# A fused attention and two-MLP kernel: the lower words of 22 weight slots, several half-precision copies and the first value splits on GpSimd, and a new order

## The chip, the cores and the metric

The kernel runs on one core of a Trainium2 chip. The metric is device time in microseconds. A core has TensorE (PE in the profile), VectorE (DVE), ScalarE (ACT), GpSimd (POOL), and SyncE (SP), which issues the DMA transfers. Each engine works through its own queue of instructions in order; semaphores tie the queues together.

## The reference, cut to what matters

```
# q, k, v: (4, 8, 576, 64); window 128
scores = scale * q @ k^T + ALiBi bias, masked to 0 <= i-j < 128
attn   = softmax(scores);  x = attn @ v               # (2304, 512) after the heads are joined
h      = x @ w_in                                      # 512 -> 1024
solu   = h * softmax(h);  ln = (solu - mean) / sqrt(var + 1e-6) * g_ln
y      = ln @ w_out                                    # 1024 -> 512
h2     = y @ w2_in;  g = h2 * sigmoid(h2)              # 512 -> 2048
out    = g @ w2_out                                    # 2048 -> 512
```

The weights arrive as 64-bit floats, so each number is two 32-bit words in memory.

## The kernel before, in words

The 2304 rows are 18 blocks of 128 (index i). Two blocks are a chunk (c, nine of them). A block goes through scores (`a_qk`, TensorE, L688), row maximum (`a_max`, L714 on DVE, read from PSUM), exponential (L719, ACT), splitting of the probabilities into two half-precision parts (`a_parts`: a copy L342 on ACT or L343 on DVE, then a subtraction L354 on DVE or L355 on POOL), a transposing DMA, the product with the values (`a_av`, L773), the first MLP (`m1_in` L820, `layer_norm`, and per chunk `m1_out` L920), and per chunk the second MLP in eight steps (`m2_in` L957, a tanh L966 on ACT, L967 on DVE, a copy L969 on ACT, L970 on DVE, and `m2_out` L984).

Each product of two numbers is made of three half-precision products: high by high, high by low, low by high. That is why every operand is split in a high part (a copy) and a low part (a subtraction).

Weights fill 48 slots of 128x512 in `W`: 0 to 7 hold w_in, 8 to 15 w_out, 16 to 31 w2_in, 32 to 47 w2_out. A slot is loaded as pairs of 32-bit words into `stage` (one transfer of 512 KB, five buffers in all), then decoded to 32-bit floats (`decode`): ACT works on the higher words (L456), DVE scales the lower words to three bits (L458), and DVE joins both into `W` (L460). 46 slots go this way, two another (L464 to L468). Then TensorE and DVE find a norm, and `split_weight` scales the slot and splits it in half-precision parts: scale L347 on ACT, L348 on DVE or L350 on POOL; copy L342 or L343; subtraction L354 or L355; or, in the slots marked V in `E_W`, scale and fused subtraction L533. The values of a block are scaled and split by `v_split`: a scaled copy (L347 or L348) and a fused subtraction on DVE (L642).

The order of all of this is fixed before the program is emitted. `Sched.solve` gives every operation an engine and a place by priorities (`RANK`, `SLOPE`, `LATER`: a number for each kind of step and block), by costs written in the code, and by the strings in `PICK` that name the engine of each copy, scale and subtraction. Operations whose entry ends in True are kept apart in that plan: two such operations on DVE and POOL are never planned at once. The join L460 does not carry that mark.

Of the kernel before, what the change touches and what calls it, by code (L numbers as in the profile page):

```python
# [298 lines left out]
def fused_kernel(ctx, tc, qk, qn, kn, vt, rel, w_in, w_out, g_ln, w2_in, w2_out, out):  # L299
# [60 lines left out]
    def transpose(fn, r=(), w=(), blocks=8):  # L360
        s.op([("SP", 1294, fn, False)], r, w, dma=165 * blocks)
# [81 lines left out]
    def decode(st, slot, j):  # L443
# [4 lines left out]
        def high():  # L448
            return st[:, :, 1]
# [186 lines left out]
    def v_split(i):  # L636
# [3 lines left out]
        r = vraw[i]  # L640
        scaled(("vh", i), 512, lambda: t[:, :, 0, :], lambda: r.tile, lambda: sv.tile, [r, sv], [(t, 0)])
# [182 lines left out]
    def layer_norm(i):  # L824
# [120 lines left out]
    def m2_in(c, j):  # L945
# [18 lines left out]
        def flat(x):  # L964
# [3 lines left out]
                                              op1=ALU.mult), [t, pt], [t])  # L968
        act(512, lambda: A.activation(flat(g[:, 0]), t.tile, AF.Copy, scale=2.0 ** -16), [t], [(g, 0)])  # L969
# [77 lines left out]
    n = 0  # L1047
    for c in range(NB // 2 + 1):
# [7 lines left out]
        while n < until:  # L1056
# [12 lines left out]
RANK = {"aturn": 8190.5, "av": 1566.9, "evac": -3109.3, "exp": 5884.2, "gate": -1711.8, "in": -283.0, "in2": 763.1,  # L1069
        "load": -4397.6, "lparts": -1653.6, "max": 176.2, "max1": 339.6, "norm": -7961.4, "out": -1027.6,  # L1070
        "out2": 3298.4, "parts": -1379.1, "qk": 1402.7, "s0": -168.5, "s16": 369.8, "s32": 455.6, "s8": 3931.6,
        "share": -1605.8, "store": 2439.7, "table": -5196.2, "tav": 59.2, "tevac": -749.8, "texp": 4157.2,
        "tpar": 3201.3, "tscore": -1216.6, "tsub": 333.9, "vload": 753.3, "vnorm": -2520.6, "vsplit": 128.2,
        "w0": 1479.2, "w16": 76.9, "w32": 998.7, "w8": -63.2, "xturn": -869.5, "y": -1911.0}
SLOPE = {"aturn": 47.79, "av": -25.89, "evac": -5.68, "exp": 11.77, "gate": -21.88, "in": 36.34, "in2": -11.62,
         "load": 10.3, "lparts": 18.87, "max": -24.94, "max1": -2.34, "norm": -4.0, "out": 15.06, "out2": 30.48,
         "parts": -23.26, "qk": 32.18, "s0": 3.76, "s16": 1.95, "s32": 6.94, "s8": 26.54, "share": 17.85,
         "store": -34.37, "table": 17.51, "tav": -5.62, "tevac": 7.06, "texp": 19.15, "tpar": 25.04, "tscore": 5.66,
         "tsub": 13.31, "vload": 7.87, "vnorm": 15.99, "vsplit": 25.91, "w0": -6.05, "w16": 1.69, "w32": -8.51,
         "w8": -8.24, "xturn": 39.68, "y": -12.6}  # L1080
# [148 lines left out]
```

## Time and profile before

| what | us |
|---|---|
| median of three runs | 732.65 |
| the three runs | 731.47, 732.65, 2431.59 |
| the profiled execution, its own time | 729.44 |
| its span, first to last instruction | 727.5 |
| busy in the span: TensorE, DVE, ACT, POOL | 674.3, 444.8, 346.2, 138.5 |
| mean granted TensorE clock | 0.981 of full |

The median is that of the two runs that agree within 1.2 us and one far outlier above them. The profiled execution's own time lies 1.9 us over its span, and 3.2 us under the median.

### The profile page before, as it was taken

To read this page: it belongs to the slowest core of one execution; us is meant where nothing else is said; L and a number is where in the kernel's file an instruction comes from. 1 tells how busy PE (TensorE), PEld (TensorE's weight loads), DVE (VectorE), ACT (ScalarE), POOL (GpSimd) and SP (SyncE) were. 2 spreads that over 40 slices of the span, in tenths; PEclk is the share of its full clock that TensorE was granted. 3 is DMA by queue.
4 is the path that set the end of the run, shared out by engine and by line. 5 is a ranking of instruction groups with operands and counts; after the bars stand their busy time and mean duration, and the time that the engine had idled before them with its cause. 6 is when DMAs were issued, how large, how long until landed. Compare 5 with 4: busy or idle time off the path is not lost.

```text
span 727.5 us, 13956 instructions
## 1 busy us (share of the span) xinstructions
PE 674.3 (93%) x5541; PEld 464.0 (64%) x5541; DVE 444.8 (61%) x1125; ACT 346.2 (48%) x738; POOL 138.5 (19%) x140
## 2 busy tenths in 40 slices
PE   4563688999999999999999999999999999999997
PEld 2432367778565577667766676678566777657853
DVE  3899999996897747553556657547672523321220
ACT  5687668575646635444454445525341422231231
POOL 1223034322443312130322112101010200100000
PEclk9996799999999999999999999999999999999999
DMA  9999985593535534251723454334250421100000
GB/s 309 346 247 273 241 199 134 131 231 89 99 78 103 130 73 81 53 114 31 145 59 73 82 107 90 91 56 73 44 102 1 68 65 30 30 30 1 1 30 29
DMA packets 142209, 75.82 MB, mean 104 GB/s; under 512 B 126656, under 2 KB 126784, under 8 KB 142144
## 3 DMA queue, kind: packets, MB, share of 16 engines
q1 hardware_dynamic: 142144, 74.94, 44.2%
q8 instruction: 43, 0.70, 0.4%
q14 instruction: 22, 0.18, 0.1%
HBM read 39.52 MB, written 4.72 MB: 61 GB/s over the span
## 4 chain that ended last, share of the span: by engine, by line
PE 79%; DVE 14%; ACT 3%; issue 2%; DMA 1%; POOL 0%; DVEq 0%; POOLq 0%; ACTq 0%
PE mm L984 25%; PE mm L957 23%; PE mm L920 12%; PE mm L820 11%; PE sa L688 4%; DVE W L460 3%; PE mm L773 2%; DVE stage L458 2%; DVE e L714 1%; PE gram L396 1%; DVE W L533 1%; PE sa L773 1%; DVE W L354 1%; DMA aT<-a 1%; DVE W L348 1%
## 5 line engine op out<-in xcount | busy, mean ns | idle before, releaser
L957 PE MATMUL mm<-y,W 128*128 128x256 f16 x1728 | 210.4, 273 | 1.1 <-DVE t L967 0.7
L984 PE MATMUL mm<-W,g 128*128 128x512 f16 x864 | 204.9, 379 | 0.0
L957 PEld LDWEIGHTS <-W 128*128 128x128 f16 x1728 | 167.0, 98 | 39.8 <-issue 2.0
L984 PEld LDWEIGHTS <-g 128*128 128x128 f16 x864 | 81.8, 98 | 78.7 <-issue 0.2
L820 PE MATMUL mm<-W,xT 128*128 128x512 f16 x432 | 105.2, 390 | 1.7 <-DVE xT L569 1.0
L920 PE MATMUL mm<-lnT,W 128*128 128x256 f16 x864 | 104.8, 273 | 0.0
L920 PEld LDWEIGHTS <-W 128*128 128x128 f16 x864 | 84.0, 98 | 19.7 <-issue 0.5
L719 ACT ACTIVATE e<-e,mx 128x256 f32<-128x256 f32 (+1 forms) x144 | 70.0, 487 | 45.9 <-DVE mx L714 43.3
L970 DVE SCALAR_TENSOR_TENSOR g<-t,g 128x512 f16<-128x512 f32 x72 | 55.5, 774 | 53.7 <-ACT g L969 53.3
L355 POOL TENSOR_TENSOR a<-e,a 128x512 f16<-128x512 f32 (+1 forms) x45 | 54.9, 1222 | 143.2 <-ACT a L342 65.8
L969 ACT ACTIVATE g<-t 128x512 f16<-128x512 f32 x72 | 45.0, 626 | 72.6 <-PE mm L984 61.1
L967 DVE SCALAR_TENSOR_TENSOR t<-t,mm 128x512 f32<-128x512 f32 x72 | 48.7, 682 | 48.3 <-ACT t L966 48.3
L966 ACT ACTIVATE t<-mm,cs 128x512 f32<-128x512 f32 x72 | 48.1, 680 | 62.5 <-PE mm L957 58.6
L820 PEld LDWEIGHTS <-xT 128*128 128x128 f16 x432 | 42.7, 100 | 47.6 <-issue 4.6
L688 PE MATMUL sa<-k,q 64*128 64x128 f32 x544 | 49.4, 312 | 17.1 <-DVE mx L714 12.2
L714 DVE CUSTOM_DVE_ANT_0 e<-sa,table 128x256 f32<-128x256 f32 (+1 forms) x144 | 53.9, 400 | 11.3 <-PE sa L688 6.3
L688 PEld LDWEIGHTS sa<-k,q 64*128 64x128 f32 x544 | 38.5, 202 | 29.1 <-DVE mx L714 15.7
L928 DVE SCALAR_TENSOR_TENSOR y<-mm,cs,y 128x512 f16<-128x512 f32 x18 | 13.3, 748 | 57.1 <-ACT y L925 57.1
L834 DVE TENSOR_REDUCE lnst<-mm 128x1 f32<-128x1024 f32 x18 | 22.0, 1220 | 42.0 <-PE mm L820 42.0
L848 POOL TENSOR_SCALAR lnst<-lnst 128x1 f32<-128x1 f32 x17 | 3.5, 203 | 214.0 <-ACT mm L845 214.0
L925 ACT ACTIVATE y<-mm,cs 128x512 f16<-128x512 f32 x18 | 12.2, 686 | 64.0 <-PE mm L920 56.3
L773 PEld LDWEIGHTS <-aT 128*128 128x128 f16 x816 | 32.9, 101 | 15.2 <-issue 8.6
(151 smaller groups left out, 707.9 us busy)
## 6 DMA issues: line engine op xcount, KB each, us to landing
stage<-in_moe_w_in_dram SPq DMA_DIRECT2D x24, 512.0 KB, 5.3
stage<-in_moe_w_out_dram SPq DMA_DIRECT2D x24, 512.0 KB, 4.5
k<-in_kn_dram SPq DMA_DIRECT2D x18, 256.0 KB, 2.9
q<-in_qn_dram SPq DMA_DIRECT2D x18, 256.0 KB, 3.1
vraw<-in_vt_dram SPq DMA_DIRECT2D x18, 256.0 KB, 3.8
out_dram<-t SPq DMA_DIRECT2D x18, 256.0 KB, 2.3
aT<-a SPq DMA_TRANSPOSE x72, 3.3
lnT<-ln SPq DMA_TRANSPOSE x34, 3.2
```

The source lines that it names most:

```text
L355: ("G", cg(n), lambda: G.tensor_tensor(dst(), a(), b(), op), True)], r, w, pick=pick)
L688: T.matmul(SA[:, j, off + sl * P:off + (sl + 1) * P], q[rows, p, :], k[rows, p, :], start=True, stop=sl not in blank)
L714: v(n + 20, lambda j=j: V.tensor_tensor_reduce(e[:, j, lo:lo + n], SA[:, j, off + lo:off + lo + n], table[:, 2 * p + j, o:o + n], -0.125, ...
L719: act(n, lambda j=j: A.activation(e[:, j, lo:lo + n], e[:, j, lo:lo + n], AF.Exp, bias=mx[:, j:j + 1], scale=-1.0, accum_out=rs[:, 2 * p + ...
L773: T.matmul(heads(i)[:, h // 4, h % 4, :], t[:, (2 * ha + j) * nh + c, :], vb[sl][:, h, hv, :], start=(n == 0), stop=(n == 3 * nh - 1))
L820: T.matmul(pt[:, half * 512:(half + 1) * 512], x[:, hx, k, :], W16(2 * k + half, hw), start=(k == 0 and hx + hw == 0), stop=(k == KD - 1 a ...
L920: T.matmul(pt[:, ct % 2], W16(8 + k, hw)[:, ct * P:(ct + 1) * P], l[:, hx * KF1 + k, :], start=(k == 0 and hw + hx == 0), stop=(k == KF1 - ...
L957: T.matmul(pt[:, mm], W16(16 + 4 * k + m // 4, hw)[:, (m % 4) * P:(m % 4 + 1) * P], y[:, hx, k, :], start=(k == 0 and hw + hx == 0), stop= ...
L966: act(512, lambda: A.activation(t.tile, flat(pt.tile), AF.Tanh, scale=cs[:, 0:1]), [pt, (cs, 0)], [t], extra=1)
L967: v(512, lambda: V.scalar_tensor_tensor(out=t.tile, in0=t.tile, scalar=1.0, in1=flat(pt.tile), op0=ALU.add, op1=ALU.mult), [t, pt], [t])
L970: v(512, lambda: V.scalar_tensor_tensor(out=flat(g[:, 1]), in0=t.tile, scalar=2.0 ** -16, in1=flat(g[:, 0]), op0=ALU.mult, op1=ALU.subtrac ...
L984: T.matmul(pt.tile, g[:, hg, mm, b * P:(b + 1) * P], W16(32 + m, hw), start=(m == 0 and hg + hw == 0), stop=(m == KF2 - 1 and hg == 1))
```

## The change

The lower words may be scaled by GpSimd (L461 of the changed kernel): the string `wd` gives 22 slots to it, one of which is in the pair that is decoded the other way, so 21 instructions move. Copies to half precision may go to GpSimd as a multiplication by one (L344): 21 of them do. The values of blocks 0 to 5 are split in three steps instead of two: scaled in place, copied, subtracted, most of it on GpSimd. A branch for the gate is added and not used (`GATE` is all V). All numbers of the order are new; some engines in `PICK`, `ROOT`, `NORM` and `E_W` are, too, and `V_AT` starts the norms of the third and fourth batch at blocks 6 and 8, not 9 and 10. Costs in the plan change with them. TensorE's instructions are the same ones, 10245 in both.

```diff
     def copy(pick, n, dst, src, r, w):
 
         s.op([("A", ca(n), lambda: A.activation(dst(), src(), AF.Copy), False),
-              ("V", cv(n, True), lambda: V.tensor_copy(dst(), src()), True)], r, w, pick=pick)
+              ("V", cv(n, True), lambda: V.tensor_copy(dst(), src()), True)] +
+             ([("G", cg1(n), lambda: G.tensor_scalar(dst(), src(), 1.0, 1.0, ALU.mult, ALU.mult), True)]
+              if pick[0] in ("wh", "ah", "xh", "lh", "vg") else []), r, w, pick=pick)
...
-            v(512, lambda: V.tensor_scalar(low(), low(), 2.0 ** -29, 7.0, ALU.mult, ALU.min), [(st, 0)],
-              [(st, "low")], fast=True)
-            v(530, lambda: V.scalar_tensor_tensor(out=out(), in0=high(), scalar=3, in1=low(),
+            s.op([("V", cv(615, True), lambda: V.tensor_scalar(low(), low(), 2.0 ** -29, 7.0, ALU.mult, ALU.min), True),
+                  ("G", cg1(560), lambda: G.tensor_scalar(low(), low(), 2.0 ** -29, 7.0, ALU.mult, ALU.min), True)],
+                 [(st, 0)], [(st, "low")], pick=("wd", j))
+            v(582, lambda: V.scalar_tensor_tensor(out=out(), in0=high(), scalar=3, in1=low(),
                                                   op0=ALU.logical_shift_left, op1=ALU.bitwise_or),
...
+        if V_SPLIT[i] == "G":
+            scaled(("vc", i), 512, lambda: r.tile, lambda: r.tile, lambda: sv.tile, [r, sv], [r], True)
+            copy(("vg", i), 512, lambda: t[:, :, 0, :], lambda: r.tile, [r], [(t, 0)])
+            combine(("vl", i), 512, ALU.subtract, lambda: t[:, :, 1, :], lambda: r.tile, lambda: t[:, :, 0, :],
+                    [r, (t, 0)], [(t, 1)])
+            return
...
-RANK = {"aturn": 8190.5, "av": 1566.9, "evac": -3109.3, "exp": 5884.2, "gate": -1711.8, "in": -283.0, "in2": 763.1,
+RANK = {"aturn": 7491.5, "av": 1875.4, "evac": -3132.7, "exp": 6823.8, "gate": -2780.3, "in": -507.5, "in2": 1352.2,
...
+PICK = {"vc": "AVVGAAAAAAAAAAAAAA", "vg": "GGAAGVAAAAAAAAAAAA", "vl": "GGGGGVGGGGGGGGGGGG",
...
+        "wd": "VVVVGVVVGGGVGVGVGVGVGVGVGVGVGVGVGVGVGVGVGVGGGVVV",
...
+V_SPLIT = "GGGGGGVVVVVVVVVVVV"
+GATE = "VVVVVVVVV"
 V_NORM = "PPAA"
-V_AT = [0, 1, 9, 10]
+V_AT = [0, 1, 6, 8]
```

How the order moves is shown at three places. The lines of the changed kernel are shifted: its L460 scales lower words on DVE, L461 on POOL, L463 joins, L350 scales, L356 and L357 subtract, L723 is the row maximum, L976 the step that was L967.

DVE, the first weights and values, before (`stage` is a loaded slot, `vraw` the values of a block, `vs` their parts):

```order
L458 TENSOR_SCALAR stage_76<-stage_76 128x512
L642 SCALAR_TENSOR_TENSOR vs_150<-vraw_170,sv0_160,vs_150 128x8x64
L642 SCALAR_TENSOR_TENSOR vs_149<-vraw_169,sv0_160,vs_149 128x8x64
L460 SCALAR_TENSOR_TENSOR W_188<-stage_76 128x512
L458 TENSOR_SCALAR stage_82<-stage_82 128x512
L460 SCALAR_TENSOR_TENSOR W_188<-stage_82 128x512
L458 TENSOR_SCALAR stage_230<-stage_230 128x512
L460 SCALAR_TENSOR_TENSOR W_188<-stage_230 128x512
```

DVE, the same place in the changed kernel:

```order
L350 TENSOR_SCALAR vraw_171<-vraw_171,sv0_160 128x512
L350 TENSOR_SCALAR vraw_170<-vraw_170,sv0_160 128x512
L586 COPY sv_4_94<-sv0_160 64x1
L463 SCALAR_TENSOR_TENSOR W_188<-stage_81 128x512
L460 TENSOR_SCALAR stage_76<-stage_76 128x512
L460 TENSOR_SCALAR stage_82<-stage_82 128x512
L463 SCALAR_TENSOR_TENSOR W_188<-stage_76 128x512
L463 SCALAR_TENSOR_TENSOR W_188<-stage_82 128x512
L460 TENSOR_SCALAR stage_77<-stage_77 128x512
L463 SCALAR_TENSOR_TENSOR W_188<-stage_77 128x512
L343 CAST a16_351<-e_247 128x256
L463 SCALAR_TENSOR_TENSOR W_188<-stage_223 128x512
```

The fused value subtractions are gone from DVE, and the join of `stage_223` has no scaling ahead of it on DVE.

POOL, from its first subtraction on, before (`a16` are parts of probabilities, `e` the probabilities, `x16` and `xm` the joined heads):

```order
L355 TENSOR_TENSOR a16_138<-e_145,a16_138 128x256
L355 TENSOR_TENSOR a16_359<-e_254,a16_359 128x256
L350 TENSOR_SCALAR W_188<-W_188,swin_155 128x512
L355 TENSOR_TENSOR a16_463<-e_376,a16_463 128x512
L355 TENSOR_TENSOR a16_482<-e_385,a16_482 128x512
L355 TENSOR_TENSOR x16_133<-xm_134,x16_133 128x512
```

POOL, the same stretch in the changed kernel, up to the scaling of a w_in slot:

```order
L357 TENSOR_TENSOR vs_149<-vraw_169,vs_149 128x8x64
L344 TENSOR_SCALAR vs_150<-vraw_170 128x8x64
L357 TENSOR_TENSOR vs_150<-vraw_170,vs_150 128x8x64
L461 TENSOR_SCALAR stage_223<-stage_223 128x512
L357 TENSOR_TENSOR a16_351<-e_247,a16_351 128x256
L461 TENSOR_SCALAR stage_359<-stage_359 128x512
L461 TENSOR_SCALAR stage_377<-stage_377 128x512
L344 TENSOR_SCALAR a16_473<-e_384 128x512
L352 TENSOR_SCALAR W_188<-W_188,swin_155 128x512
```

Two subtractions stood before the scaling of that slot; now there are thirteen instructions, of which the last eight are shown.

DVE at the seventh step L967 of the second MLP, before (the joins around it are those of the last weight slots):

```order
L714 ISA e_1941,mx_1602<-sa_75,table_187 128x256
L714 ISA mx_1602 128x1
L458 TENSOR_SCALAR stage_1886<-stage_1886 128x512
L468 SCALAR_TENSOR_TENSOR W_188<-stage_1820,W_188 128x512
L967 SCALAR_TENSOR_TENSOR t_1723<-t_1723,mm_1910 128x512
L460 SCALAR_TENSOR_TENSOR W_188<-stage_1886 128x512
```

DVE at the seventh such step in the changed kernel (its L976):

```order
L723 ISA e_2029,mx_1888<-sa_75,table_187 128x256
L723 ISA mx_1888 128x1
L976 SCALAR_TENSOR_TENSOR t_1782<-t_1782,mm_1953 128x512
L792 TENSOR_SCALAR rinv_1452<-rsum_896 128x8
L793 RECIPROCAL rinv_1452<-rinv_1452 128x8
L467 TENSOR_SCALAR W_188<-stage_1991 128x512
L469 SCALAR_TENSOR_TENSOR W_188<-stage_1991,W_188 128x512
L471 SCALAR_TENSOR_TENSOR W_188<-stage_1991,W_188 128x512
L976 SCALAR_TENSOR_TENSOR t_1793<-t_1793,mm_2021 128x512
```

The last of these L976 is the seventh. In both orders all but the last joins of weights stand ahead of it, and nearly the same number of matrix products that can start before it: 894 before, 910 in the change.

## Rows read from the trace of the kernel before

**Rows 1.** The page, busy tenths in 40 slices of the span: TensorE and DVE.

```profile
PE   4563688999999999999999999999999999999997
DVE  3899999996897747553556657547672523321220
```

**Rows 2.** Stretches: us, then busy us (instructions) by engine, granted clock, DMA share, GB/s.

```profile
0.00:20.00 20.00, 7.87 (x53) 5.72 (x53) 8.30 (x38) 12.37 (x33) 2.42 (x15) 1.00 0.97 313
20.00:160.00 140.00, 103.44 (x911) 72.81 (x911) 134.57 (x340) 99.18 (x205) 40.83 (x38) 0.90 0.85 225
160.00:700.00 540.00, 539.28 (x4462) 373.74 (x4463) 297.18 (x741) 228.32 (x492) 95.28 (x87) 1.00 0.34 69
700.00:727.00 27.00, 23.70 (x122) 11.73 (x120) 4.74 (x7) 6.31 (x10) 0.00 (x0) 1.00 0.10 39
```

**Rows 3.** Waits: engine line <- releaser: us in total, times, longest.

```profile
PE sa L688 <- DVE mx L714: 12.2, 11, 3.9
...
PE mm L773 <- DMA aT<-a: 0.5, 1, 0.5
...
DVE e L714 <- PE sa L688: 1.6, 2, 1.3
```

**Rows 4.** Order of time, 155 to 166 us, DVE and TensorE: start, us, what.

```profile
160.01 0.67 DVE L967 SCALAR_TENSOR_TENSOR t<-t,mm 128x512 f32<-128x512 f32 x1
...
161.23 0.82 PE L920 MATMUL mm<-lnT,W 128*128 128x256 f16 x6
```

**Rows 5.** DVE by line and form, 0 to 160 us: count, busy us, mean ns.

```profile
L460 DVE SCALAR_TENSOR_TENSOR W<-stage 128x512 uint32<-128x512 uint32 x44 | 34.5, 795 | 0.9 <-ACT stage L456 0.4
L458 DVE TENSOR_SCALAR stage<-stage 128x512 uint32<-128x512 uint32 x45 | 21.7, 489 | 0.0
L714 DVE CUSTOM_DVE_ANT_0 e<-sa,table 128x256 f32<-128x256 f32 x34 | 13.5, 413 | 2.8 <-PE sa L688 1.6 <-PE sa L773 1.2
L354 DVE TENSOR_TENSOR W<-W 128x512 f16<-128x512 f32 x10 | 8.2, 816 | 0.0
L533 DVE SCALAR_TENSOR_TENSOR W<-W,sw2in 128x512 f16<-128x512 f32 x6 | 5.8, 986 | 0.4 <-ACT W L347 0.4
...
L642 DVE SCALAR_TENSOR_TENSOR vs<-vraw,sv,vs 128x512 f16<-128x512 f32 x5 | 3.6, 739 | 0.0
...
L343 DVE CAST a<-e 128x512 f16<-128x512 f32 x6 | 3.3, 543 | 0.0
```

**Rows 6.** The tiles W and stage: duration ns min/median/max, first and last start.

```profile
L460 DVE SCALAR_TENSOR_TENSOR W<-stage x46: 670/680/2049, 16.0 to 167.1; 128x512 uint32<-128x512 uint32 x46
L354 DVE TENSOR_TENSOR W<-W x16: 673/679/1666, 40.4 to 222.8; 128x512 f16<-128x512 f32 x16
L355 POOL TENSOR_TENSOR W<-W x16: 1152/1162/2067, 46.6 to 211.4; 128x512 f16<-128x512 f32 x16
L533 DVE SCALAR_TENSOR_TENSOR W<-W,sw2in x6: 734/747/1640, 115.6 to 140.3; 128x512 f16<-128x512 f32 x6
L348 DVE TENSOR_SCALAR W<-W,sw2out x6: 473/478/887, 178.6 to 206.4; 128x512 f32<-128x512 f32 x3, 128x512 f16<-128x512 f32 x3
...
L458 DVE TENSOR_SCALAR stage<-stage x46: 367/417/1380, 15.4 to 166.2; 128x512 uint32<-128x512 uint32 x46
```

**Rows 7.** POOL's one-input scaling L350: duration ns min/median/max, first and last start.

```profile
L350 POOL TENSOR_SCALAR W<-W,sw2in x2: 848/848/849, 107.7 to 108.6; 128x512 f32<-128x512 f32 x2
L350 POOL TENSOR_SCALAR W<-W,swin x1: 1088/1088/1088, 33.2 to 33.2; 128x512 f32<-128x512 f32 x1
L350 POOL TENSOR_SCALAR W<-W,gs x1: 686/686/686, 59.9 to 59.9; 128x512 f32<-128x512 f32 x1
```

**Rows 8.** Order of time from 107.4 to 110.4 us, POOL and DVE.

```profile
107.75 1.68 POOL L350 TENSOR_SCALAR W<-W,sw2in 128x512 f32<-128x512 f32 x2 [0.79 <-DVE q L1024]
...
108.07 1.63 DVE L348 TENSOR_SCALAR W<-W,sw2in 128x512 f32<-128x512 f32 x2
```

More of the change, by code (lines that the diff above doesn't have):

```diff
@@ L360, in transpose @@
     def transpose(fn, r=(), w=(), blocks=8):
[L361 removed]
+        s.op([("SP", 1340, fn, False)], r, w, dma=165 * blocks)
     W = Buf(const, [P, NSLOT + LAG, 512], F32, "W")
@@ L849, in layer_norm @@
                                                                ALU.add), False)], [st], [st])
-            s.op([("G", 500, lambda: G.tensor_tensor(y(), var(), half.tile, ALU.pow), False)], [st, half], [st])
+            s.op([("G", 600, lambda: G.tensor_tensor(y(), var(), half.tile, ALU.pow), False)], [st, half], [st])
         else:
@@ L968, in m2_in @@
                                               op1=ALU.mult), [t, pt], [t])
+        if GATE[c] == "G":
+            s.op([("G", cg1(512), lambda: G.tensor_scalar(t.tile, t.tile, 2.0 ** -16, 1.0, ALU.mult, ALU.mult), True)], [t], [t])
+            act(512, lambda: A.activation(flat(g[:, 0]), t.tile, AF.Copy), [t], [(g, 0)])
+            combine(("gl", 8 * c + j), 512, ALU.subtract, lambda: flat(g[:, 1]), lambda: t.tile, lambda: flat(g[:, 0]),
+                    [t, (g, 0)], [(g, 1)])
+            return
         act(512, lambda: A.activation(flat(g[:, 0]), t.tile, AF.Copy, scale=2.0 ** -16), [t], [(g, 0)])
@@ L1068 @@
 PITCH = 3.3
-RANK = {"aturn": 8190.5, "av": 1566.9, "evac": -3109.3, "exp": 5884.2, "gate": -1711.8, "in": -283.0, "in2": 763.1,
[L1070 to L1080, printed above, removed]
@@ new lines @@
+RANK = {"aturn": 7491.5, "av": 1875.4, "evac": -3132.7, "exp": 6823.8, "gate": -2780.3, "in": -507.5, "in2": 1352.2,
+        "load": -2824.7, "lparts": -3034.5, "max": 84.6, "max1": 392.4, "norm": -8853.1, "out": -1490.3,
+        "out2": 3717.9, "parts": -2273.7, "qk": 3081.3, "s0": -306.0, "s16": 481.0, "s32": 328.1, "s8": 2710.1,
+        "share": -2261.1, "store": 1605.4, "table": -4240.8, "tav": -557.6, "tevac": -1278.1, "texp": 3785.6,
+        "tpar": 2319.1, "tscore": -1263.8, "tsub": -212.9, "vload": 44.4, "vnorm": -3148.1, "vsplit": 223.5,
+        "w0": 2109.6, "w16": 57.9, "w32": 1362.9, "w8": -131.9, "xturn": -879.3, "y": -2860.6}
@@ new lines @@
+SLOPE = {"aturn": 47.89, "av": -22.61, "evac": -14.72, "exp": -2.87, "gate": -24.33, "in": 25.61, "in2": -11.6,
+         "load": 28.66, "lparts": 27.36, "max": -22.88, "max1": -16.17, "norm": 22.54, "out": 15.38, "out2": 35.04,
+         "parts": -16.75, "qk": 33.9, "s0": 10.1, "s16": -14.11, "s32": 9.76, "s8": 3.0, "share": -4.92,
+         "store": -24.87, "table": 14.8, "tav": 16.37, "tevac": 14.98, "texp": 13.48, "tpar": 20.69, "tscore": 10.69,
+         "tsub": 26.39, "vload": 10.76, "vnorm": 13.38, "vsplit": 28.36, "w0": 2.86, "w16": 12.75, "w32": 0.21,
+         "w8": -9.8, "xturn": 21.02, "y": -16.83}
```

98 lines of the change are left out of this document (49 added, 49 removed), and 41 rows, old and new, of the table LATER.

## The prediction

> **What bounds the kernel now.** I read the slices of the page first, then stretches of the span, then the waits, then the DVE groups of the first stretch. In the slices [rows 1] TensorE is at 9 tenths or more from the eighth slice to the last but one; DVE is at 9 in slices three to nine and falls to half and less later. The stretches give that in numbers [rows 2]: from 160 to 700 us TensorE is busy 539.28 of 540 us, and of its waits there the longest is 0.5 us, for a transposing DMA [rows 3]. So the last 567 us are TensorE's, its instructions are the same in both kernels, and nothing that happens on other engines there can shorten them. The time is decided by when TensorE becomes full. From 20 to 160 us it is busy 103.44 of 140 us while DVE is busy 134.57 of 140 [rows 2], and its largest wait is for DVE's row maxima, 12.2 us [rows 3]; DVE's own largest wait in that stretch is 1.6 us [rows 3]. **DVE bounds the first 160 us.**
>
> A landmark ties this to the two orders: the seventh step L967 of the second MLP, which DVE ended at 160.01 + 0.67 = 160.68 us; 0.55 us later TensorE goes on with `m1_out` and does not starve again [rows 4]. In both orders all but the last weight joins stand ahead of this step, and 894 and 910 matrix products can start before it, so it is the same point of the work. How much earlier DVE gets there is what the change is worth; the 567 us behind it are added unchanged, the last 3.3 us without TensorE (27.00 less 23.70, rows 2) too.
>
> **The change on DVE up to the landmark.** Counted in the two orders, with durations that no neighbour stretched.
> - Lower words: 45 become 23, at the median of 417 ns [rows 6]: 22 x 0.417 = -9.2 us (21 go to POOL, one moves behind the landmark).
> - Fused value subtractions: 5 become 0, at 739 ns [rows 5]: -3.7 us.
> - Value scalings on DVE: one becomes two, at 473 ns [rows 6]: +0.5 us.
> - Probability parts: one subtraction more, at some 0.68 us as L354 [rows 6], two copies fewer, at most 0.54 us each [rows 5] and, one of them being of half size, some 0.7 us in all: 0.
> - Row maxima: six more of 413 ns [rows 5] stand ahead of the landmark, with the reading of the result that follows each, together 3.0 us. This is block work that is moved forward.
>
> Sum: -9.2 - 3.7 + 0.5 + 3.0 = **-9.4 us**. ScalarE was busy 99.18 of 140 us [rows 2] and up to the landmark it loses nine instructions (copies, value scalings, one decoding step) and gains twelve of like size (six of them exponentials): nothing, covered by its 40 idle us; without that cover the three that are over.
>
> **The change on POOL up to the landmark.** The form of the 21 lower words, 32-bit whole numbers with a step of two, doesn't appear on POOL in the trace. The nearest rows are the one-input scalings L350, 686 ns alone and up to 1088 ns [rows 7]; I take 0.69, since the longer ones lie beside DVE work, and 1.09 is the other end (8.4 us more of POOL). 21 x 0.69 = 14.5; ten copies of full size at 0.69 = 6.9 and two of half size at some 0.45 = 0.9; five value subtractions at 1.16 [rows 6] = 5.8; two more probability subtractions, 2.3. One value scaling comes and one weight scaling goes. **Together +30.4 us**, on an engine that was busy 2.42 + 40.83 = 43.3 us of these 160 [rows 2]. It has room; the question is what it does to DVE.
>
> **What POOL costs DVE.** L460 takes 680 ns at the median, 2049 at most [rows 6], and 795 in the mean of this stretch [rows 5]. L458 takes 417 and 489, L354 679 and 816, L533 747 and 986. The row maximum, which reads PSUM, is not stretched: 413 mean. In order of time the stretched ones lie beside POOL: two scalings L348 took 1.63 us together while two L350 ran [rows 8], against 2 x 0.473 alone [rows 6], 0.68 us more. So a DVE operation between SBUF tiles waits until the one on POOL ends. What was lost that way: L460 44 x (795 - 680) = 5.1 us, L458 45 x 72 = 3.2, L354 10 x 137 = 1.4, L533 6 x 239 = 1.4: 11.1 us, for 43.3 us of POOL, or 0.26 us for each us of POOL. L460 alone, the one group that the plan does not keep apart from POOL, lost 5.1 / 43.3 = 0.12. So the new 30.4 us of POOL cost DVE between 30.4 x 0.12 = 3.6 us (the plan keeps the others apart) and 30.4 x 0.26 = 7.9 (they collide as the old ones did). The nearest rows to the new instructions are the four L350 of this stretch: 0.68 us lost beside two of them, nothing noted beside the others, in 1.70 + 1.09 + 0.69 = 3.5 us [rows 7, 8], 0.2. I take 30.4 x 0.2 = **+6.1 us**.
>
> The Trainium skill has the rule behind this: "SBUF — State Buffer", section "SBUF: two separate sides", says that VectorE and GpSimd hold one pair of ports as an exclusive lock for a whole instruction, and "Perfetto Trace Analysis", section "Optimizing Scalar/DVE Operations", warns that moving work between these two "might not help". The trace agrees on the lock (0.68 us lost beside L350). Taken to its end, with every new us of POOL kept from DVE, the rule would turn -3.3 into +21.0 us; by the rows it stays at -3.3.
>
> **What else is moved.** The joins of 21 slots now wait for POOL as well as for ScalarE. Behind a waiting join stands all of DVE, and behind that TensorE's scores and norms. Cover: in the new order POOL's lower word stands several DVE instructions ahead of its join (the join of stage 223 is the last of the twelve rows shown of the new order). I cost it at 0; without the cover a join waits for one POOL subtraction and the scaling, 1.16 + 0.69 us, at most, which for a fifth of the 21 would be 8 us. SP's queue keeps its transfers and gets a new order; DVE waited for no load in the rows, so 0, with the weights' loads as what comes next if DVE runs ahead.
>
> **Sum.** -9.4 + 6.1 = -3.3 us. On the profiled execution: 729.44 - 3.3 = 726.1, with a span near 724. That execution lies 3.2 us under the median of the runs, and the measurement is one of runs: 732.65 - 3.3 = **729.3 us**, 0.5% less. A change of under 2% (14.7 us) is about what a measurement of this kernel can't tell from none.
>
> **Rivals.**
> 1. *POOL's work hides.* The plan puts the new instructions where DVE reads PSUM, and no further us is lost. For it: row maxima, reductions and the MLP steps on PSUM are not stretched, and of POOL's 43.3 us before, 32 delayed none of the groups above. Against: L460, 30 us of the stretch, isn't kept apart. Time: 732.65 - 9.4 = 723.3; if part of the 11.1 us lost now goes as well, with a third of it, 719.6. Chance 0.26.
> 2. *The shared access becomes the bound* (slower). Before, DVE's groups that stretch (L460 29.9 us, L458 18.8, L354 6.8, L533 4.5, L642 3.6, L343 2.5, unstretched) and POOL's 43.3 make 109 us of 160. After, 109 - 13 + 30 = 127 in a stretch that should be 151 long. It decides from the point where DVE pays more than 9.4 / 30.4 = 0.31 us for each us of POOL; if it pays all of it, the loss is 30.4 - 9.4 = 21.0. Halfway, +10.5: 743. For it: the lock leaves only 24 us for everything that has to line up, on two engines whose queues can't be reordered. Against: at today's 0.26 it is not reached. By the skill's rule, an exclusive lock, this is the case if the plan does not hold in time. Chance 0.17.
> 3. *Joins wait for POOL.* The price above, 8 us, turns -3.3 into +4.7: 737. For it: POOL's queue had two subtractions ahead of the first w_in scaling and now has thirteen instructions. Against: POOL is busy 74 us of 151. Chance 0.07.
>
> **How the numbers follow.** Forecast 0.50 (726 to 733, the two bounds of POOL's price: 732.65 - 9.4 + 3.6 = 726.9 and + 7.9 = 731.2, with 1 us of scatter between runs, as 731.47 and 732.65 show). Rival 1 reaches from 714 to 724, rival 2 from 735 to 753, rival 3 from 733 to 741. The range 718 to 742 leaves out the lower third of rival 1 and the upper half of rival 2, under 0.2 together. Faster by over 2%, under 718.0: that third of rival 1 and a little of the forecast, 0.11. Slower by over 2%, over 747.3: a third of rival 2, 0.06. Within: 0.83.
>
> **What would show it.** Right: TensorE without waits from about 157 us on; the seventh of the former L967 ending near 157; joins (L463) with a mean above 795 ns; POOL busy over 70 us up to there; lower words on POOL near 0.7 us where DVE reads PSUM. Wrong if DVE shows idle time before the joins with POOL as releaser (rival 3), if joins and scalings on DVE show means far above 1 us (rival 2), if their means fall to 700 or less (rival 1), or if a lower word on POOL takes over 1.1 us by itself, which no row here excludes. It would also be wrong if the new order made TensorE wait behind the landmark, where it now waits under 1 us.

## The result and the profile after

The changed kernel takes **741.0 us** (median of four runs, 738.67 to 743.59); the kernel before, beside it, 732.28 us. The ratio is 1.0124, 95% interval [1.0081, 1.0167]: 8.7 us slower, within 2% but beyond what these runs leave in doubt. (One of the four runs of before took 2431.59 us; the ratio leaves it out, and the median of the other three, 731.92, makes the difference 9.1 us.) The profiled execution took 741.23 us with a span of 739.5.

Here are the slices of the page, busy tenths in 40 slices of the span, for the engines of [rows 1], and with them GpSimd and TensorE's granted clock:

```profile
PE   3554669889999999999999999999999999999997
...
DVE  3898899887599745753658468466572432422220
...
POOL 2686667744256121130314022100110200100000
PEclk9995589989999999999999999999999999999999
```

TensorE is full from the tenth slice on, where it was full from the eighth. In the fourth and fifth slices its granted clock stands at 5 tenths, near the lower of its two levels, 1.2 GHz, after three slices in which it was busy 3 to 5 tenths; in the kernel before, those two slices read 6 and 7.

The same in stretches of the span (us, then busy us and instructions of PE, PEld, DVE, ACT and POOL, granted clock, DMA share, GB/s), cut at the landmark:

```profile
0.00:20.00 20.00, 7.20 (x49) 5.23 (x49) 7.87 (x34) 12.12 (x32) 6.86 (x21) 1.00 0.91 298
20.00:174.80 154.80, 109.18 (x951) 77.44 (x951) 136.88 (x331) 103.33 (x214) 104.18 (x73) 0.86 0.77 210
160.00:700.00 540.00, 538.94 (x4502) 376.90 (x4500) 303.65 (x760) 232.50 (x498) 108.26 (x96) 1.00 0.36 73
```

And the kernel before, from 20 us to its landmark:

```profile
20.00:160.68 140.68, 104.12 (x920) 73.33 (x919) 135.25 (x342) 99.51 (x206) 40.83 (x38) 0.90 0.85 225
```

The landmark, the seventh step of the second MLP (now L976), in order of time:

```profile
174.12 0.68 DVE L976 SCALAR_TENSOR_TENSOR t<-t,mm 128x512 f32<-128x512 f32 x1
```

It ends at 174.80 us, 14.1 us after the 160.68 of before [rows 4]. Behind it nothing has happened: TensorE is busy 538.94 of 540 us (539.28 before, [rows 2]), and what lies between the landmark and the end of the span fell from 727.5 - 160.68 = 566.8 to 739.5 - 174.80 = 564.7 us. So the whole loss is ahead of the landmark; since the rest is 2.1 us shorter, the landmark stands that much further on in the work of the new order, and 14.1 counts 2.1 too many. (The profiled execution of before took 729.44 us, 2.8 under its median here; so 12.0 us between the spans stand beside 8.7 between the medians.)

Of the two columns that count there, DVE is busy about as long as before, 136.88 us against 135.25; its idle time went from 140.68 - 135.25 = 5.4 to 154.80 - 136.88 = 17.9 us. The lower clock, 0.86 in this stretch against 0.90, is not what costs the time: a kernel of the next section has 0.86 there too and does not lose. GpSimd's work up to the landmark went from 2.42 + 40.83 = 43.3 us ([rows 2] and the stretch above) to 6.86 + 104.18 = 111.0 us: **+67.8**, not +30.4.

What makes it so long stands in the rows of the tile `stage` (duration in ns, least, median, most):

```profile
L463 DVE SCALAR_TENSOR_TENSOR W<-stage x46: 672/692/1643, 18.0 to 182.8; 128x512 uint32<-128x512 uint32 x46
L460 DVE TENSOR_SCALAR stage<-stage x25: 368/422/1375, 16.0 to 182.3; 128x512 uint32<-128x512 uint32 x25
...
L461 POOL TENSOR_SCALAR stage<-stage x21: 1975/2049/2506, 21.4 to 167.7; 128x512 uint32<-128x512 uint32 x21
```

A lower word on GpSimd takes 2049 ns at the median and never under 1975. DVE's waits from 20 us to the landmark (us in total, times, longest) name GpSimd, which had no such row before:

```profile
DVE W L463 <- POOL stage L461: 4.5, 5, 1.9
...
DVE W L343 <- POOL W L357: 1.3, 1, 1.3
DVE e L723 <- POOL a L357: 1.1, 1, 1.1
```

With three more (1.1, 0.7 and 0.5 us) DVE waits 9.2 us for results of GpSimd, of which the joins are half.

And in order of time around 42 us, first GpSimd, then DVE (start, duration, what, in brackets the idle time before it and its releaser):

```profile
41.55 7.20 POOL L461 TENSOR_SCALAR stage<-stage 128x512 uint32<-128x512 uint32 x3
```

```profile
41.67 1.12 DVE L356 TENSOR_TENSOR W<-W 128x512 f16<-128x512 f32 x1
43.62 1.73 DVE L463 SCALAR_TENSOR_TENSOR W<-stage 128x512 uint32<-128x512 uint32 x2 [0.83 <-POOL stage L461]
45.27 0.68 DVE L356 TENSOR_TENSOR W<-W 128x512 f16<-128x512 f32 x1
46.20 0.69 DVE L463 SCALAR_TENSOR_TENSOR W<-stage 128x512 uint32<-128x512 uint32 x1 [0.25 <-POOL stage L461]
```

Three lower words stand in a row on GpSimd, 7.2 us of them; DVE does what it can, then stands 0.83 and 0.25 us before the joins of these slots, and all that is queued behind the joins with it.

### The profile page after: what moved, and what is told of

Read it like the earlier page. It is cut to its first block, busy times and chain, and to the rows that moved or that the text cites. A ratio compares the mean times of both kernels' runs of the same rounds, so it can differ in the third digit from the quotient of the medians.

```text
span 739.5 us, 13994 instructions
## 1 busy us (share of the span) xinstructions
PE 677.1 (92%) x5539; PEld 467.0 (63%) x5541; DVE 442.6 (60%) x1099; ACT 346.8 (47%) x732; POOL 208.4 (28%) x182
## 4 chain that ended last, share of the span: by engine, by line
PE 78%; DVE 5%; POOL 4%; ACT 3%; issue 1%; POOLq 0%; DVEq 0%
PE mm L999 25%; PE mm L966 25%; PE mm L929 11%; PE mm L829 10%; PE sa L697 4%; PE mm L782 2%; POOL stage L461 1%; POOL W L357 1%; DVE e L723 1%; DVE W L463 1%; PE sa L782 1%; ACT e L728 1%; ACT stage L458 0%; DVE ln L343 0%; POOL a L357 0%
## 5 line engine op out<-in xcount | busy, mean ns | idle before, releaser
L985 DVE SCALAR_TENSOR_TENSOR g<-t,g 128x512 f16<-128x512 f32 x72 | 57.2, 795 | 58.3 <-ACT g L984 58.0
L357 POOL TENSOR_TENSOR a<-e,a 128x512 f16<-128x512 f32 (+1 forms) x43 | 54.8, 1276 | 83.7 <-DVE a L343 44.1
L976 DVE SCALAR_TENSOR_TENSOR t<-t,mm 128x512 f32<-128x512 f32 x72 | 48.9, 682 | 49.0 <-ACT t L975 49.0
L697 PE MATMUL sa<-k,q 64*128 64x128 f32 x544 | 51.0, 319 | 23.6 <-DVE mx L723 16.0
L723 DVE CUSTOM_DVE_ANT_0 e<-sa,table 128x256 f32<-128x256 f32 (+1 forms) x144 | 53.8, 401 | 17.4 <-PE sa L697 12.1
L461 POOL TENSOR_SCALAR stage<-stage 128x512 uint32<-128x512 uint32 x21 | 44.7, 2130 | 10.6 <-ACT stage L458 5.3
L463 DVE SCALAR_TENSOR_TENSOR W<-stage 128x512 uint32<-128x512 uint32 x46 | 39.7, 872 | 5.9 <-POOL stage L461 4.5
```

The costliest lines, as they stand in the source:

```text
L357: ("G", cg(n), lambda: G.tensor_tensor(dst(), a(), b(), op), True)], r, w, pick=pick)
L461: ("G", cg1(560), lambda: G.tensor_scalar(low(), low(), 2.0 ** -29, 7.0, ALU.mult, ALU.min), True)],
L697: T.matmul(SA[:, j, off + sl * P:off + (sl + 1) * P], q[rows, p, :], k[rows, p, :], start=True, stop=sl not in blank)
L723: v(n + 20, lambda j=j: V.tensor_tensor_reduce(e[:, j, lo:lo + n], SA[:, j, off + lo:off + lo + n], table[:, 2 * p + j, o:o + n], -0.125, ...
L976: v(512, lambda: V.scalar_tensor_tensor(out=t.tile, in0=t.tile, scalar=1.0, in1=flat(pt.tile), op0=ALU.add, op1=ALU.mult), [t, pt], [t])
L985: v(512, lambda: V.scalar_tensor_tensor(out=flat(g[:, 1]), in0=t.tile, scalar=2.0 ** -16, in1=flat(g[:, 0]), op0=ALU.mult, op1=ALU.subtrac ...
```

## The experiments

All ratios are against runs of the kernel before on the same chip, whose median there was 732.2 to 732.4 us. Six kernels, those of the second and third question below, keep the changed kernel's order and alter one form, or the engine of some instructions at the places where they stand; those are the ones that tell causes apart.

**Why is a lower word 2 us long?** The theories were the 32-bit whole numbers, the step of two words, and the neighbour on DVE. The first kernel adds scalings to the changed kernel's last chunk, where DVE has little to do, on a tile of zeros of its own:

```diff
+            pr = Buf(const, [P, FF1], F32, "e1", N_E1)
...
+            for fn in (
+                lambda: G.tensor_scalar(even(U32), even(U32), 2.0 ** -29, 7.0, ALU.mult, ALU.min),
+                lambda: G.tensor_scalar(even(F32), even(F32), 2.0 ** -29, 7.0, ALU.mult, ALU.min),
+                lambda: G.tensor_scalar(flat(U32), flat(U32), 2.0 ** -29, 7.0, ALU.mult, ALU.min),
+                lambda: G.tensor_scalar(flat(F32), flat(F32), 2.0 ** -29, 7.0, ALU.mult, ALU.min),
...
+                lambda: G.tensor_scalar(even(U32), even(U32), 2.0 ** -29, 1.0, ALU.mult, ALU.mult),
```

> The changed kernel with 24 more GpSimd scalings on a tile of zeros in the last chunk, three of each of eight forms, where GpSimd has nothing else to do. Theory A (the lower words cost what they do because the words are whole numbers): the form of the change, 32-bit whole numbers with a step of two, takes 2.0 us as in the changed kernel, the same on floats 0.7 us, and whole numbers without a step 2.0 us too. Theory B (the step of two costs it): floats with a step of two take 2.0 us, whole numbers without a step 0.7. Theory C (the neighbours on VectorE stretch it): every form takes 0.7 us alone. The time of the whole is that of the changed kernel, 741 us, by all of them, since GpSimd's queue ends there.

Measured, by line of that kernel in the order of the lines shown (`even` is every second word, `flat` 512 in a row; ns least, median, most):

```profile
L1005 POOL TENSOR_SCALAR e<-e x3: 1989/2002/2016, 634.3 to 638.5; 128x512 uint32<-128x512 uint32 x3
L1006 POOL TENSOR_SCALAR e<-e x3: 1981/1992/1997, 640.5 to 644.7; 128x512 f32<-128x512 f32 x3
L1007 POOL TENSOR_SCALAR e<-e x3: 1917/1918/1919, 646.7 to 650.7; 128x512 uint32<-128x512 uint32 x3
L1008 POOL TENSOR_SCALAR e<-e x3: 1918/1918/1919, 652.7 to 656.7; 128x512 f32<-128x512 f32 x3
L1012 POOL TENSOR_SCALAR e<-e x3: 646/650/653, 677.9 to 679.4; 128x512 uint32<-128x512 uint32 x3
```

None of the three: floats, whole numbers, spread or in a row, all take 1.9 to 2.0 us with hardly a neighbour. (The three forms whose rows are left out, with mixed types and signed numbers, have medians of 1.99 us.) The last row has the same operands as the first and takes 650 ns. What differs is the pair of operations: multiplication and **minimum** against two multiplications. The time of the kernel, 741.2 us, did not move.

A second kernel of the kind tries other pairs, on 512 floats with a step of two:

```diff
+                lambda: G.tensor_scalar(even(F32), even(F32), 0.5, 7.0, ALU.mult, ALU.min),
+                lambda: G.tensor_scalar(even(F32), even(F32), 0.5, 7.0, ALU.mult, ALU.max),
+                lambda: G.tensor_scalar(even(F32), even(F32), 7.0, 0.5, ALU.min, ALU.mult),
+                lambda: G.tensor_scalar(even(F32), even(F32), 0.5, 7.0, ALU.add, ALU.min),
+                lambda: G.tensor_scalar(even(F32), even(F32), 7.0, None, ALU.min),
+                lambda: G.tensor_scalar(even(F32), even(F32), 0.5, 7.0, ALU.mult, ALU.add),
+                lambda: G.tensor_scalar(even(F32), even(F32), 0.5, 7.0, ALU.add, ALU.mult),
+                lambda: G.tensor_scalar(even(F32), even(F32), 0.5, None, ALU.mult),
```

> The changed kernel with 24 more scalings on GpSimd in the last chunk, on 512 floats of value zero, three each of eight pairs of operations. Theory D (the minimum is the slow operation): (mult, min), (min, mult), (add, min) and a single min take 1.9 to 2.1 us each, (mult, max) too; (mult, add), (add, mult) and a single mult take 0.6 to 0.8 us. Rival E (only two multiplications together are quick, any other second operation is slow): (mult, add) and (add, mult) take 2.0 us as well. Rival F (a minimum is slow only as the second operation): (min, mult) and the single min take 0.65 us. The time of the kernel itself stays at 741 plus or minus 3 us, since the last chunk is TensorE's.

```profile
L1005 POOL TENSOR_SCALAR e<-e x3: 1986/2005/2005, 633.1 to 637.2; 128x512 f32<-128x512 f32 x3
L1006 POOL TENSOR_SCALAR e<-e x3: 1992/1996/2015, 639.3 to 643.5; 128x512 f32<-128x512 f32 x3
L1007 POOL TENSOR_SCALAR e<-e x3: 1995/1997/2533, 645.6 to 649.7; 128x512 f32<-128x512 f32 x3
L1008 POOL TENSOR_SCALAR e<-e x3: 1994/2010/2012, 652.3 to 656.5; 128x512 f32<-128x512 f32 x3
L1009 POOL TENSOR_SCALAR e<-e x3: 1557/1580/1595, 658.6 to 661.9; 128x512 f32<-128x512 f32 x3
L1010 POOL TENSOR_SCALAR e<-e x3: 647/648/971, 663.6 to 665.4; 128x512 f32<-128x512 f32 x3
L1011 POOL TENSOR_SCALAR e<-e x3: 647/648/650, 666.1 to 667.6; 128x512 f32<-128x512 f32 x3
L1012 POOL TENSOR_SCALAR e<-e x3: 1552/1612/1992, 668.3 to 672.1; 128x512 f32<-128x512 f32 x3
```

Theory D holds for pairs: the four tried with a minimum or maximum take 2.0 us, with the minimum in either place (F falls), and pairs of multiplication and addition take 0.65 (E falls). It fails for one operation alone: a single multiplication takes 1.55 to 1.99 us, no less than a single minimum. What is quick in these rows is not "no minimum" but "two operations, both multiplication or addition". The kernel took 740.1 us.

**Is that length the loss?** First with GpSimd's lower words as a quick pair that writes zeros (they read a constant, so three low bits of these weights are lost):

```diff
-  G.tensor_scalar(low(), low(), 2.0 ** -29, 7.0, ALU.mult, ALU.min)
+  G.tensor_scalar(low().bitcast(F32), half.tile.to_broadcast([P, 512]), 0.0, 0.0, ALU.mult, ALU.add)
...
```

> The changed kernel with the same order on every engine; the 21 lower-word instructions on GpSimd write floats of zero from a constant in place of scaling whole numbers, so the lowest three bits of those weights are left out. Theory A (the length of this instruction is what turned the forecast over): each takes 0.7 us or less, GpSimd's time up to the seventh gate step falls from 112 us to about 84, the seventh step ends near 158 us instead of 174.8, and the whole lands at the sum of the prediction, 729 us (727 to 732). Rival (the number of instructions that need the shared access, not their length, holds VectorE back): 736 us or more. Rival (the new order is the loss): 739 to 741.

Measured 731.77 us, ratio 0.9989 [0.9975, 1.0004]: 9.2 us come back. The time is in theory A's range, though the seventh step ended at 165.66 us and not near 158. Then with full words as input, one factor more in place of the minimum:

```diff
-  G.tensor_scalar(low(), low(), 2.0 ** -29, 7.0, ALU.mult, ALU.min)
+  G.tensor_scalar(low(), low(), 1.75 * 2.0 ** -30, 1.0, ALU.mult, ALU.mult)
```

> The changed kernel with one thing altered: the lower words on GpSimd are scaled by one factor (1.75 x 2 to the -30) and then by 1.0 and have no minimum, so the last three bits of these weights are rounded otherwise; the order on all engines stays that of the changed kernel. If the length of the instruction is the loss: each takes 0.65 us, GpSimd does about 83 us up to the seventh gate step, and the time is 731.8 (730.5 to 733), as with the zeros. If the zeros of that earlier run had helped in another way (no read of the stage tile): 735 to 741.

Measured **731.59 us**, ratio 0.9984 [0.9969, 0.9998], so the zeros had not helped in another way. Its stretches, the group of lower words on GpSimd, and DVE's joins and own lower words up to 160 us (count, busy us, mean ns, idle before and releaser):

```profile
0.00:20.00 20.00, 7.08 (x48) 5.11 (x49) 7.76 (x34) 12.14 (x32) 6.74 (x21) 1.00 0.91 298
20.00:164.98 144.98, 110.02 (x951) 78.13 (x950) 134.45 (x331) 102.75 (x214) 77.20 (x73) 0.86 0.86 222
```

```profile
L461 POOL TENSOR_SCALAR stage<-stage 128x512 uint32<-128x512 uint32 x21 | 19.8, 943 | 14.6 <-ACT stage L458 5.4 <-DVE accw2in L403 2.2 <-DVE mx L723 1.9
```

```profile
L463 DVE SCALAR_TENSOR_TENSOR W<-stage 128x512 uint32<-128x512 uint32 x42 | 37.4, 901 | 1.1 <-ACT stage L458 0.8
...
L460 DVE TENSOR_SCALAR stage<-stage 128x512 uint32<-128x512 uint32 x23 | 12.6, 556 | 0.0
```

GpSimd does 6.74 + 77.20 = 83.9 us up to this landmark (27 us less than the changed kernel), and no instruction of DVE waits for its results. The landmark is at 165.00 us. The changed kernel reaches it 9.8 us later in the same order: DVE is busy 2.5 us longer (144.75 against 142.21 from the start) and idle 7.3 us longer, and its waits for GpSimd are 9.2 us against none. The granted clock is 0.86 in both.

Between the two lengths lies the single multiplication:

```diff
-  G.tensor_scalar(low(), low(), 2.0 ** -29, 7.0, ALU.mult, ALU.min)
+  G.tensor_scalar(low(), low(), 1.75 * 2.0 ** -30, None, ALU.mult)
```

> The changed kernel, same order on all engines, its lower words on GpSimd scaled with one multiplication alone and no minimum (the last three bits of these weights are rounded otherwise); in the last-chunk measurement one multiplication alone took 1.55 to 1.99 us against 0.65 for a pair of multiplications and 2.0 for multiplication and minimum. If the time goes with the length of this instruction: 731.6 + 9.4 x (1.6 - 0.65)/(2.05 - 0.65) = 738 (736 to 740). If it is the minimum that hurts in another way, or only lengths over some step: 731 to 733.

Measured 736.0 us, ratio 1.0044 [1.0031, 1.0057]: the lower end of the first theory's 736 to 740.

```profile
20.00:169.81 149.81, 108.19 (x954) 76.34 (x953) 138.94 (x331) 102.87 (x214) 94.23 (x73) 0.87 0.82 215
```

```profile
L461 POOL TENSOR_SCALAR stage<-stage 128x512 uint32<-128x512 uint32 x21 | 35.8, 1707 | 10.6 <-ACT stage L458 5.0 <-DVE lnT L572 2.6 <-DMA stage<-in_moe_w_out_dram 1.2
```

```profile
L463 DVE SCALAR_TENSOR_TENSOR W<-stage 128x512 uint32<-128x512 uint32 x42 | 37.3, 897 | 2.2 <-POOL stage L461 1.3 <-ACT stage L458 0.5
L460 DVE TENSOR_SCALAR stage<-stage 128x512 uint32<-128x512 uint32 x23 | 14.6, 640 | 0.0
```

So with everything else in place, 19.8, 35.8 and 44.7 us of lower words on GpSimd give 731.6, 736.0 and 741.0 us: 0.28 us for each us first, then 0.56, by the medians. (The interval of the 741.0 reaches 3 us to either side, so the two prices may lie closer together.) The stretches show a difference between the two parts: from 19.8 to 35.8 us DVE becomes busier (134.45 to 138.94) and its idle time stays (144.98 - 134.45 = 10.5, 149.81 - 138.94 = 10.9); from 35.8 to 44.7 DVE is not busier (136.88) and idles 17.9 us. First its instructions are stretched, its own lower words above all (556 to 640 ns; the joins stay at 901 and 897), then it waits for results.

**What is the moved work worth on DVE, in the same order?** The 21 lower words alone back on DVE, at the places where the plan had them for GpSimd:

```diff
-  G.tensor_scalar(low(), low(), 2.0 ** -29, 7.0, ALU.mult, ALU.min)
+  V.tensor_scalar(low(), low(), 2.0 ** -29, 7.0, ALU.mult, ALU.min)
```

> The changed kernel's order with the 21 lower words back on VectorE, each where the plan had it for GpSimd. Theory A: VectorE gets 21 x 0.42 = 8.8 us back and GpSimd loses 43 us; against the kernel before, VectorE does 0.5 us less up to the seventh gate step (-9.4 + 8.8) and GpSimd 16 us more at 0.2 us lost for each, 3 us: 732 + 2.6 = 735 us. Rival (the shared access, by number): 733. Rival (the new order is the loss): 740.

Measured 731.34 us, ratio 0.9989 [0.9976, 1.0001], below all three theories: moving the lower words to GpSimd in their quick form (731.59) gained nothing. Then the copies, value scaling and value subtractions back instead, with the quick lower words on GpSimd:

```diff
-  G.tensor_scalar(dst(), src(), 1.0, 1.0, ALU.mult, ALU.mult)
+  V.tensor_copy(dst(), src())
...
-  G.tensor_tensor(dst(), a(), b(), op)
+  (V if pick[0] == "vl" else G).tensor_tensor(dst(), a(), b(), op)
...
```

> The order of the changed kernel with the quick lower words (two multiplications, last three bits rounded otherwise) on GpSimd, and its 12 copies to half precision and 5 subtractions of value splitting back on the vector engine at the same places. If the vector engine's time sets the seventh gate step and each us of GpSimd costs it 0.2: + 12 x 0.3 + 5 x 0.68 - 16 x 0.2 = + 4, 735 to 736 against 731.6. If these copies hid nothing, the time is 731 to 732; if GpSimd beside the vector engine costs more than the moved work is worth, 728 to 730.

Measured 731.44 us, ratio 0.9982 [0.9972, 0.9992], where 735 to 736 was expected from the vector engine's time. Its stretches:

```profile
0.00:20.00 20.00, 7.21 (x49) 5.24 (x49) 8.43 (x40) 12.15 (x32) 3.06 (x16) 1.00 0.92 298
20.00:165.00 145.00, 108.47 (x952) 76.72 (x951) 135.73 (x343) 103.06 (x214) 61.85 (x59) 0.88 0.86 223
```

GpSimd does 3.06 + 61.85 = 64.9 us up to this landmark, at 165.00, instead of 83.9; from the start DVE is busy 8.43 + 135.73 = 144.16 us instead of 142.21, only 2 us more with eighteen rows more. That the 19 us that GpSimd no longer does beside it paid for the rest of their time is the likely reading. And everything back on DVE, which leaves the new order alone (the edits of the two kernels above together):

> The order of the changed kernel alone: lower words, copies and value subtractions that it moved to GpSimd are all on the vector engine, at the places where the plan had them. If the moved work is worth what the sum says (vector engine 8.8 + 3.6 + 3.4 = 15.8 us longer, 30 us of GpSimd less, of which 0.2 comes back): + 9.8 to the 731.6 of the quick form, 741. If each move is worth nothing net, as lower words alone were (731.3 on the vector engine, 731.6 on GpSimd): 731 to 733. If the new order is itself worth something to the kernel: below 730.

Measured 733.17 us, ratio 1.0004 [0.9987, 1.0020]: the second of its three cases. The order by itself costs nothing that can be measured, and the work moved by quick instructions gains 1.6 us by the medians, with intervals that overlap: little or nothing, and not 10. Its stretches and groups, from an execution of 729.17 us, 4.0 under its median, so that its landmark at 162.49 is early too:

```profile
0.00:20.00 20.00, 7.47 (x49) 5.24 (x49) 8.65 (x42) 12.31 (x32) 2.43 (x15) 1.00 0.95 300
20.00:162.49 142.49, 105.54 (x950) 75.39 (x951) 135.90 (x363) 103.31 (x215) 47.18 (x39) 0.89 0.85 226
```

```profile
L463 DVE SCALAR_TENSOR_TENSOR W<-stage 128x512 uint32<-128x512 uint32 x44 | 33.2, 765 | 1.1 <-ACT stage L458 0.9
...
L460 DVE TENSOR_SCALAR stage<-stage 128x512 uint32<-128x512 uint32 x23 | 10.5, 462 | 0.0
L461 DVE TENSOR_SCALAR stage<-stage 128x512 uint32<-128x512 uint32 x21 | 8.8, 418 | 0.0
```

Beside the quick form, DVE is busy 144.55 - 142.21 = 2.3 us longer from the start although it does 8.8 us of lower words more, and 9.6 us of copies, subtractions and one scaling. Much of the difference is in its other rows: joins 765 ns here and 901 there (42 x 0.136 = 5.7 us), its own lower words 462 and 556 ns (23 x 0.094 = 2.2 us). With 49.6 us of GpSimd they are stretched less than with 83.9.

**The same with the order planned anew.** The kernel before with only the 21 lower words on GpSimd:

```diff
-            v(512, lambda: V.tensor_scalar(low(), low(), 2.0 ** -29, 7.0, ALU.mult, ALU.min), [(st, 0)],
-              [(st, "low")], fast=True)
+            s.op([("V", cv(512, True), lambda: V.tensor_scalar(...), True),
+                  ("G", cg1(560), lambda: G.tensor_scalar(...), True)], [(st, 0)], [(st, "low")], pick=("wd", j))
...
```

> The kernel before with only the 21 lower words given to GpSimd, planned anew with its own numbers of order. Theory A (2.05 us each, 43 us of GpSimd more in a stretch of 140): VectorE does 8.8 us less and waits more, by what the changed kernel showed (10 us of stretching and 13 of idle time for 68 us of GpSimd, so about 0.34 for each): 732 - 8.8 + 14.6 = 738 us, slower. Rival (the new order, the copies or the value splits are the loss): 732 or less.

Measured 759.44 us, ratio 1.0389 [1.0361, 1.0417], worse than all theories; DVE's joins (L461 in this kernel) waited for GpSimd more than in the changed kernel:

```profile
DVE W L461 <- POOL stage L459: 9.2, 6, 4.2
```

With the quick pair instead:

> The kernel before with the lower words of the same 21 weight slots on GpSimd, planned anew by its own tables, in the form of two multiplications at 0.65 us instead of multiplication and minimum. If the length was what made this 759.4: 21 x 1.4 us of GpSimd work go, and the time falls to between 727 and 734 (vector engine 9 us shorter, 21 x 0.65 x 0.2 = 2.7 us of it given back, some idle time between 0 and 6). If it was the old order, in which the joins wait for GpSimd whatever its speed: it stays above 740.

Measured 754.18 us, ratio 1.0305 [1.0286, 1.0324]: a miss. These two kernels have one plan, the same on every engine, and in it the length is worth 5.3 of the 27 us; the joins' wait fell to the last row below (up to 180 us), and other waits, for ScalarE and TensorE, stand ahead of it:

```profile
...
DVE t L968 <- ACT t L967: 6.6, 3, 4.2
DVE lnst L835 <- PE mm L821: 3.9, 2, 3.5
DVE W L461 <- POOL stage L459: 3.6, 3, 2.9
```

The tables of ranks are those found for the kernel before, and the plan that they give with other costs is another one on every engine. Which of its moves costs the other 22 us was not tried. The last kernel met the same: it is the changed kernel with the quick lower words, and it tells the plan that the join, too, holds the access that DVE and GpSimd share.

```diff
-              [(st, "low"), (st, "high")], w)
+              [(st, "low"), (st, "high")], w, port=True)
```

> The quick lower words (two multiplications), and the plan told that the join of the two words holds the shared access as well, so that it sets joins and GpSimd's work apart where it can; the order is planned anew. If the joins are stretched by GpSimd beside them and the plan can prevent it: the mean join falls from 0.87 to 0.75 us, 44 x 0.1 = 4 to 5 us come off, 727 to 730. If the order's ranks, found for the unmarked join, suit the new plan badly: 734 to 745. If joins do not share the access: 731 to 733 with the mean join unchanged.

```profile
L463 DVE SCALAR_TENSOR_TENSOR W<-stage 128x512 uint32<-128x512 uint32 x44 | 33.7, 777 | 1.5 <-POOL stage L461 0.5 <-POOL lnst L857 0.4 <-issue 0.2
```

Measured 777.53 us, ratio 1.0608 [1.0582, 1.0634]. The first theory was right on the join, whose mean fell from 901 to 777 ns, 42 x 0.124 = 5 us; the second was right on the direction of the time, which went far beyond its 734 to 745. Part of the fall may be that GpSimd does less there, 69.7 us in the first 160 against 81.5; but with 64.9 and 64.2 us up to the landmark, copies or lower words back on DVE, the joins of the unmarked plan still took 836 and 863 ns. So a plan that keeps the two apart does shorten the joins. Whether that pays could not be seen: the seventh step ends at 229.79 us, with DVE busy only 170.40 of the 209.79 us from 20 us to there, and ranks found for another plan are the likely reason.

## Why the prediction was wrong, point by point

- **What bounds, and the landmark: right.** The loss lies ahead of the seventh step L976 (14.1 us there, 12.0 in the spans), and the rest is TensorE's as said, if 2.1 us shorter. (The wait of 12.2 us for row maxima is that of the first 160 us; from 20 us on it is 9.4.)
- **"21 x 0.69 = 14.5": the step that failed.** The price of a lower word on GpSimd was read from L350 [rows 7], a scaling by two multiplications, because it has one input and the same size. Whole numbers and the step were named as the unknown; the operations were not, and they were the difference. It measured 44.7 us for the 21, beyond the upper end of 1.09 us each too, 30.2 us over the price, and with other work that took longer too the sum for GpSimd was +67.8 us rather than +30.4. "Over 1.1 us by itself" stands in the prediction's last list; that price had no place in the range or the chances.
- **Joins waiting for GpSimd at 0: failed with it.** DVE waited 4.5 us in five waits before joins, and 9.2 us for GpSimd's results in all. The length alone, at the prediction's own 0.2 to 0.26 for each us, would have made -9.4 us into +4.2 to +8.2; the traces show a smaller part as longer work (DVE busy 1.2 us more than before, where -9.4 was counted) and 12.9 us as idle time. That the wait comes from the length, and not from where the plan put the instruction, is shown by the same order with the quick pair, where none of these waits is left. It is rival 3's mechanism. Rival 2's point, 0.31 us of DVE for each us of GpSimd, was passed as well: (14.1 + 9.4) / 67.8 = 0.35, but the last part of it as idle time and not as stretched instructions.
- **The signs it asked for:** GpSimd over 70 us (111.0) and joins over 795 ns (871 up to 160 us) came, the end of the step near 157 us and lower words near 0.7 us did not. Of its signs of being wrong two came: DVE idle before joins with GpSimd as releaser, and lower words over 1.1 us.
- **The price of 0.2 us for each us of GpSimd: about right.** The quick form has 83.9 - 43.3 = 40.7 us of GpSimd more than before, 10.3 beyond the 30.4; half of that is its lower words, which take 641 ns at the least and 943 in the mean. By the prediction's own sum that is -9.4 + 40.7 x 0.2 = -1.3 us; DVE was indeed busy 1.3 us less up to the landmark (142.21 against 143.55), and the time was -0.7 by the medians, -2.3 to -0.1 by the interval. That the time agrees so well is in part luck: the landmark itself came at 165.00 us, not 1.3 us before 160.68, for DVE idled 5.7 us more; against that the two profiled executions lie 2.1 us apart (731.58 and 729.44), and the rest behind the landmark is 2 us shorter. Had the instruction been as priced, the forecast of 729.3 would have been some 2 us low.
- **The term of -9.4 us on DVE: right as a count, not as a gain.** From the start up to the landmark DVE was busy 143.55 us before, 144.55 with all the work on it, 142.21 with the quick form and 144.75 in the changed kernel. What is taken off comes back in the rows that stay. Some of it was never there: the durations overlap, as two rows of the quick form show, where a lower word of 0.42 us is followed 0.34 us later:

```profile
45.91 0.42 DVE L460 TENSOR_SCALAR stage<-stage 128x512 uint32<-128x512 uint32 x1
46.25 0.68 DVE L356 TENSOR_TENSOR W<-W 128x512 f16<-128x512 f32 x1
```

  If all of them lie like these two, 22 free 7.5 us rather than 9.2.

The loss adds up in one order: the new order 732.4 to 733.2, the moved work in quick instructions -1.6 to 731.6, the minimum +9.4 to 741.0. Only the last step is clear of the scatter between runs.

The rule of the Trainium skill that the prediction weighed, an exclusive lock on one pair of ports ("SBUF — State Buffer", section "SBUF: two separate sides"), agrees with the joins as far as they go: 765, 901 and 777 ns with 49.6 us of GpSimd, with 83.9, and with a plan that keeps them apart. They do not lengthen further with GpSimd's time, 871 ns with the 111.0 us of the changed kernel; there DVE waits instead. The skill's other sentence, that moving work between these two engines "might not help" ("Perfetto Trace Analysis", section "Optimizing Scalar/DVE Operations"), is what 733.2 against 731.6 us shows, a difference within the scatter, with 83.9 - 49.6 = 34.3 us of GpSimd spent on it.

## What to carry to other kernels

Price an instruction that an engine has not yet run by a row with the same operations, not only the same size and type, and if there is none, run it alone first: three of them in an idle stretch told 2.0 from 0.65 us. Between DVE and GpSimd count what comes back as stretched neighbours and late results; here 18.4 us of durations taken off DVE left its busy time up to the landmark 2.3 us shorter. And where an order is tuned by tables, compare causes within one order: with the same quick instructions, plans made anew from old tables took 22 us more than the kernel before, and 46 more than the changed order, and which of their moves did it stays open.

## What the hardware showed unexpectedly

- On GpSimd `tensor_scalar` over 512 elements took 0.65 us as a pair of multiplication and addition or two multiplications, 1.9 to 2.0 us in the pairs tried with a minimum or maximum, and 1.55 to 2.0 us with one operation alone. Writing a scaling as a pair with a 1.0 is so the quicker way, by a factor of more than two.
- Whole numbers or floats and a step of one or two words changed the medians of the pair of multiplication and minimum by less than 0.1 us.
